# Half of the early tokens' first layer in seven products, and a new order of small transfers, in a routed-expert kernel

## The chip, the cores and the metric

The kernel runs on one core of a Trainium2 chip. The metric is device microseconds (us) of one execution; the kernel before took 435.68 us (median of 3 runs, 435.34 to 438.09). The profile names the engines PE (TensorE: matmuls and transposes), PEld (its weight loads), DVE (VectorE), ACT (ScalarE), POOL (GpSimd) and SP (SyncE, which only starts transfers). Each engine works through its own instructions in a fixed order; a `q` behind a name (SPq) is that engine's queue of transfers.

## The reference

Two blocks follow one another. The first is a linear attention with decay over 4 batches, 8 heads, 768 positions and head size 64, in blocks of positions with a running state. Its output is laid out as 3072 tokens of 512 numbers. The second sends each token to one of 8 experts:

```python
logits = x @ w_gate
expert_idx = np.argmax(logits, axis=1)
...
for e in range(E):
    mask = expert_idx == e
    ...
    xe = x[mask]
    h = np.maximum(xe @ w1[e], 0.0)      # 512 -> 1024
    ye = h @ w2[e]                       # 1024 -> 512
    out[mask] = gate_w[mask, None] * ye
```

All of it is in float32. The number of tokens of each expert is known only when the attention has run.

## The kernel before, in words

**Attention.** Twelve steps: six blocks of 128 positions, times two pairs of batches. Each step turns q and k, forms scores, outputs and the new state on PE, and turns the outputs into rows of tokens that go to `xs` in DRAM (`store_rows`). One step later the step's tokens are routed: `leave` forms logits, `choose` (line 397 on) finds on DVE the best expert (`mx`, `sh`, `key`, `pick`, `oh`), `ranks` (line 441) counts on PE, with the matrix `oh`, how many tokens before a given one chose the same expert, `put` turns that into a place on the expert's list (`place`, `slot`, `slot_i`), and POOL writes an entry at that place of `slots` in DRAM (`store`, line 467): one indirect transfer for 128 tokens. These transfers wait in the list `waiting` until `store_places` issues some.

**Early tokens.** Expert 5 (`FIRST`) is begun before the lists are complete. After two thirds of the routing, POOL reads the first 256 places of its list (`list_0a`), and `gather_early` fetches those 256 rows of `xs` into `xg` with two indirect transfers. A manual dependency (`hold`) keeps the first of them until PE has done the step's scores. SP's load of the expert's second weight matrix `w2t` waits for both gathers; its `w1t` was loaded ahead in two halves.

**The experts' passes.** Pass 0 is these 256 tokens; pass 1 ("0b") is the rest of expert 5, up to 128 tokens; passes 2 to 8 are the other seven experts, in an order that depends on how many tokens each has, so that SP reads the expert's number (`turns`, made on DVE) before it can load list and weights. In each pass, tokens are turned into `xgT` (128 partitions x 4 pieces x tokens; PE transposes and a copy in passes 0 and 1, `turn`, and for the others 16-bit planes made on ACT, transposed by the DMA engines from SP's queue, and copied together again on ACT, `split` and `join`). The first layer is `hidden` (line 606: 8 blocks of 128 outputs, each four matmuls over the four pieces) for passes 0 and 1. From pass 2 on it is `hidden_fast`: a product of 2x2 blocks with seven block products instead of eight (Strassen's form, with 4 sums of weight blocks made on POOL, `s_...`, 4 sums of token blocks made on DVE, `t_...`, and sums of the products on DVE). The second layers are in seven products as well (lines 774, 782 and 914). In pass 0 DVE makes the sums of `w2t` (`second_sums`, line 683) and those of `hT` (lines 752 to 755).

**Order.** The instructions are put into each engine's order by a scheduler that estimates times; those wrapped in `pin` keep the order in which they are written. Buffers come from pools with a fixed number of rooms for a name: there is one room for `xgT`, so that the `xgT` of pass 2 can only be written when pass 1's first layer has read its own.

Of the kernel before, what the change touches and what calls it, by code (L numbers as in the profile page):

```python
# [10 lines left out]
F32 = mybir.dt.float32  # L11
# [11 lines left out]
def kernel(  # L23
# [207 lines left out]
    def pin(inst):  # L231
        tc.keep_in_program_order(inst)
        return inst
# [270 lines left out]
    def at(m, t):  # L504

        w = m.widths[t]
        return m.ids[:w, t, 0:1], m.ids[:w, t, 1:2], m.list[:w, t, 2:3]
# [76 lines left out]
        for u in range(2):  # L584
            pin(nc.scalar.copy(to[:, u], m.across[u][:, :, :m.n]))

    def turn(m, pin=lambda inst: inst):
        m.xgT = ffn.tile([P, DC, m.n], F32, tag="xgT", name="xgT", bufs=1)
        for c in range(0, DC, 2):
            tp = bank(next(tp_banks), [P, 2, m.n], "tp")  # L590
            for dc, (t, w) in itertools.product(range(c, c + 2), enumerate(m.widths)):
                pin(nc.tensor.transpose(tp[:, dc - c, t * P:t * P + w],
                                        m.xg[t // 2][:w, t % 2, dc * P:(dc + 1) * P],
                                        ident[:w, :w]))

# [15 lines left out]

    DH, FH = DC // 2, F // 2

    def form(product, sums_of, temps, give, first=nothing):

        a, b = sums_of
        p1, u2, u3 = temps
        pin(nc.scalar.copy(p1, product(a.a11, b.b11)))  # L618
        first()
        pin(nc.vector.tensor_add(u2, product(a.s2, b.t2), p1))  # L620
        pin(nc.vector.tensor_add(u3, product(a.s3, b.t3), u2))
        p5 = product(a.s1, b.t1)
        give(1, 1, p5, u3)
        nc.vector.tensor_add(u2, p5, u2)
        give(0, 0, product(a.a12, b.b21), p1)
        give(0, 1, product(a.s4, b.b22), u2)
        give(1, 0, product(a.a22, b.t4), u3)

    def form_early(product, sums_of, temps, give, ahead):

        a, b = sums_of
        p1, u2, u3, u4 = temps
        nc.vector.tensor_copy(p1, product(a.a11, b.b11))
        give(0, 0, product(a.a12, b.b21), p1)
        nc.vector.tensor_add(u2, product(a.s2, b.t2), p1)
        nc.vector.tensor_add(u3, product(a.s3, b.t3), u2)
        p5 = product(a.s1, b.t1)
        give(1, 1, p5, u3)
        nc.vector.tensor_add(u4, p5, u2)
        give(0, 1, product(a.s4, b.b22), u4)  # L640
        ahead()
        give(1, 0, product(a.a22, b.t4), u3)

    def right_sums(b, t1, t2, t3, t4, sub):
# [9 lines left out]
    def pool_sub(o, x, y):  # L654
        return nc.gpsimd.tensor_tensor(out=o, in0=x, in1=y, op=ALU.subtract)  # L655
# [130 lines left out]
    def pair_rooms():  # L786
        o = [o_room[:, next(o_slots)] for i in range(2)]
        outs = [[o[i][:, k * MD // 2:(k + 1) * MD // 2] for k in range(2)] for i in range(2)]
        u = x_room[:, next(x_slots)].rearrange("p b (i n) -> p (b i) n", i=2)
        return o, outs, [u[:, i, :] for i in range(4)]  # L790

    def outputs_early(m, w2, ahead):
        a = left_of(m.hT, 0, P, pair_rooms_of_sums())
        for make in (a.s3_made, a.s1_made, a.s2_made, a.s4_made):
            make()
        o, outs, temps = pair_rooms()

        def give(i, k, p, u):
            gate = at(m, i)[2]
            nc.vector.tensor_scalar_mul(outs[i][k], u, gate)  # L800
            nc.vector.scalar_tensor_tensor(out=outs[i][k], in0=p, scalar=gate, in1=outs[i][k],
                                           op0=ALU.mult, op1=ALU.add)

        form_early(block, (a, w2), temps, give, ahead)
        for i in range(2):
            scatter(at(m, i)[1], o[i])

    def lone_tile(m, i, b, banks):

# [325 lines left out]
    def gather_early(other):  # L1135

        m, w2t = passes[0], weights[0][1]
        pin(nc.gpsimd.memset(between, 0.0))
        begun = fetch(m, 1 + (NSTEP - 2) * B * C, pin)
        hold(begun[0], other)  # L1140
        behind = nc.sync.dma_start(out=w2t, in_=w2_r[FIRST])
        pin(behind)
        for other in begun:
            tc.add_manual_dep(behind.ins, other.ins.name, mybir.DependencyInfo(
                mybir.DependencyClass.Sync, mybir.DependencyReason.DATA),
                reason="the gathers have the DMA engines first")
# [15 lines left out]
        nc.gpsimd.tensor_copy(gates[1][halves[u]], gates[0][halves[1 - u]])  # L1162
    for i in range(len(steps)):
        rest = leave(last, (4, 6, 7) if i < len(steps) - 1 else (4, 2, 3)) if last else nothing

        ahead = (enter(i + 1, rest, stores(i))
                 if 0 < i < len(steps) - 1 else None)
        if ahead:
            if last:
                with tc.issue_after(ahead.copied.ins):  # L1170
                    store_rows(last)
        elif last:
            store_rows(last)
# [12 lines left out]
        to_sbuf(cur)  # L1186
        if cur.n == NSTEP - 1:
            if ahead:
                for s in range(2):
                    score(ahead, s)  # L1190
                gather_early(ahead.scored)
# [12 lines left out]
        for group in ranked:  # L1204
            give_places(group)
        if 0 < i < 3:
            empty_lists(i - 1)
        if ahead and i < len(steps) - 3:
            fade(ahead)
            store_places(1 if i < 5 else 2)  # L1210
        last, cur = cur, ahead
# [47 lines left out]
                           engines=[mybir.EngineType.SP])  # L1259
        passes.append(make_pass(e, 0, CAPS[i], str(i)))  # L1260

    passes.append(make_pass(FIRST, EARLY, CAPS[0] - EARLY, "0b"))
    next_pass(1)
    later = []
    weights.append(load_weights(passes[2].w, later))
    for m in passes[1:]:
        fetch(m)
    last = E
    for i in range(last + 1):
        m = passes[i]  # L1270
        w1t, w2t = weights[max(i - 1, 0)]
        ahead = passes[i + 1] if 0 < i < last else None


        def beside():
            if ahead:
                split(ahead)
                if later:
                    with tc.issue_after(ahead.turning.ins):
                        later.pop()()  # L1280

        def between():
            if waiting_rows:
                waiting_rows.pop()()

        if i == 0:
            w2 = second_sums(w2t, vector_sub)
        if i < 2:
            hidden(m, w1t)
        elif i < last:  # L1290
            w2 = across_sums(w2t)
            hidden_fast(m, w1, beside, lambda: between() or token_halves(m))
        else:
            w2 = second_sums(w2t, pool_sub_last)
            tc.keep_in_program_order(nc.gpsimd.drain())
            hidden_fast(m, w1, beside, between, TG * P)
            later_sums(m)
        if i == 0:
            split(passes[2])
            with tc.issue_after(passes[2].turning.ins):  # L1300
                for j in range(2, E):
                    next_pass(j)
            later.pop()()
        if ahead:
            w1, finish = first_sums(weights[i][0])
        if 0 < i < last - 1:
            fetch(passes[i + 2], pin=pin)
        if i == 0:
            outputs_early(m, w2, lambda: turn(passes[1], pin))
# [58 lines left out]
```

## Time and profile before

| what | us |
|---|---|
| median of 3 runs | 435.68 (435.34 to 438.09) |
| the profiled execution | 435.07 |
| its span, first to last instruction | 432.8 |
| PE busy | 421.3 (97%) |
| DVE, POOL, ACT busy | 266.0, 257.5, 176.8 |
| routing of the last steps and early first layer on PE | 118 to 140 |
| second layer of pass 0, first layer of pass 1 | 140 to 159.7 |
| second layer of pass 1 | 159.7 to 167.8 |
| passes 2 to 8 | 167.8 to 407, then a tail to 432.8 |

The times in this table and in the rows below are those of the profiled execution, counted from its first instruction. A matmul in float32 appears in the trace as two records, so "x56" of line 606 is 28 matmuls. PE's granted clock is 1.00 in all stretches from 107 to 407 us, which is the higher of its two levels (2.4 GHz).

### The profile page before, as it was taken

Reading aid. Unit: us, or ns where it says so; the run is one execution under the profiler, and the core shown is the slowest. Engines: PE = TensorE matmul, PEld = TensorE weight load, DVE = VectorE, ACT = ScalarE, POOL = GpSimd, SP = SyncE. Lnnn points to the kernel's source line nnn. Section 1 sums busy time; section 2 is a strip of 40 time slices with the busy share of each in tenths; the row PEclk is TensorE's granted clock in tenths of the full one; section 3 lists DMA queues with packets and bytes.
Section 4 is the critical chain, followed back from the end, with each engine's and each line's share of the span. In section 5 each row is a group of like instructions: output and inputs, shape, how many; then the busy total and the mean of one; then the engine's idle time right before and its main releaser. Section 6 shows DMA issues by size and latency. Waiting matters only on the chain.

```text
span 432.8 us, 9573 instructions
## 1 busy us (share of the span) xinstructions
PE 421.3 (97%) x3699; PEld 393.9 (91%) x3699; DVE 266.0 (61%) x585; ACT 176.8 (41%) x319; POOL 257.5 (59%) x205
## 2 busy tenths in 40 slices
PE   8999999999999999999999999999999999999993
PEld 6888898888888897999999999999999999999972
DVE  6656656566766647686547757755575664775463
ACT  3366545555542423450554155245424605422221
POOL 5243457373344368777948757693885887749032
PEclk9999999999999999999999999999999999999998
DMA  9999989999985758976369857965975894753122
GB/s 174 211 245 229 220 213 213 233 193 249 292 283 149 265 105 234 325 246 237 52 139 190 332 76 157 319 179 112 299 246 81 196 384 80 153 186 56 20 83 63
DMA packets 164727, 83.49 MB, mean 193 GB/s; under 512 B 146019, under 2 KB 146063, under 8 KB 164672
## 3 DMA queue, kind: packets, MB, share of 16 engines
q1 hardware_dynamic: 155024, 63.21, 61.2%
q0 software_dynamic: 5712, 13.26, 10.2%
q10 hardware_dynamic: 3936, 6.31, 4.2%
q8 instruction: 31, 0.51, 0.5%
q14 instruction: 24, 0.20, 0.2%
HBM read 58.96 MB, written 13.09 MB: 166 GB/s over the span
## 4 chain that ended last, share of the span: by engine, by line
PE 87%; DMA 4%; issue 3%; ACT 2%; POOL 1%; SPq 1%; DVE 1%; POOLq 0%; ACTq 0%
PE p L728 30%; PE p L914 26%; PE sp L279 5%; PE ph L606 5%; PE op L314 4%; PE p L774 3%; DMA v_in<-in_v_dram 3%; PE cp L340 2%; PE tx L376 2%; PE tk L241 2%; PE tq L241 2%; PE op L305 2%; PE p L782 2%; PE lgT L366 1%; DMA xg<-xs,list_0a 1%
## 5 line engine op out<-in xcount | busy, mean ns | idle before, releaser
L533 POOL DMA_INDIRECT out_dram<-o_room,list x24 | 25.7, 1069 | 51.9 <-DMA decay<-planes_q 22.4
L286 DVE TENSOR_TENSOR mt<-sp,decay 128x512 f32<-128x512 f32 x48 | 30.1, 684 | 23.8 <-PE sp L279 18.6
L739 ACT ACTIVATE hT<-hT 128x418 f32<-128x418 f32 (+6 forms) x56 | 28.3, 521 | 34.1 <-DVE hT L736 31.2
L728 PE MATMUL p<-xgT,w1t 128*128 128x209 f32 (+6 forms) x224 | 41.4, 327 | 0.0
L728 PEld LDWEIGHTS p<-xgT,w1t 128*128 128x128 f32 x224 | 37.1, 189 | 0.8 <-issue 0.8
L618 ACT COPY u_qT<-p 128x418 f32<-128x418 f32 (+6 forms) x14 | 6.7, 479 | 69.5 <-PE p L728 69.5
L914 PE MATMUL p<-hT,w2t 128*128 128x209 f32 (+5 forms) x192 | 33.6, 328 | 0.0
L914 PEld LDWEIGHTS p<-hT,w2t 128*128 128x128 f32 x192 | 32.0, 189 | 0.0
L467 POOL DMA_INDIRECT slots<-entry,slot_i x24 | 23.8, 990 | 13.1 <-PE tl L391 5.9
L527 POOL DMA_INDIRECT xg<-xs,list x25 | 25.9, 1034 | 9.0 <-issue 6.1
L736 DVE TENSOR_TENSOR hT<-p,u_kd 128x418 f32<-128x418 f32 (+6 forms) x28 | 15.6, 559 | 21.0 <-PE p L728 21.0
L279 PE MATMUL sp<-qT,kT 64*128 64x128 f32 x384 | 27.5, 293 | 0.4 <-ACT kT L263 0.4
L279 PEld LDWEIGHTS sp<-qT,kT 64*128 64x128 f32 x384 | 24.3, 199 | 3.0 <-issue 2.0
L269 POOL TENSOR_TENSOR kd<-k_in,kdec 128x512 f32<-128x512 f32 x12 | 12.4, 1042 | 23.7 <-PE cp L340 11.9
L655 POOL TENSOR_TENSOR s_q<-w1t 128x1024 f32<-128x1024 f32 x7 | 16.5, 2363 | 16.6 <-DVE t_xT L713 14.6
L326 ACT COPY xT<-op 128x512 f32<-128x512 f32 x12 | 7.0, 585 | 36.9 <-PE op L314 33.8
L606 PE MATMUL ph<-xgT,w1t 128*128 128x256 f32 (+1 forms) x128 | 21.6, 328 | 0.0
L606 PEld LDWEIGHTS ph<-xgT,w1t 128*128 128x128 f32 x128 | 19.2, 191 | 1.7
L728 PE MATMUL p<-t_sd,w1t 128*128 128x209 f32 (+6 forms) x112 | 20.7, 327 | 0.0
L728 PE MATMUL p<-st,s_q 128*128 128x209 f32 (+6 forms) x112 | 20.7, 327 | 0.0
L652 POOL TENSOR_TENSOR w1t<-w1t 128x1024 f32<-128x1024 f32 x7 | 20.2, 2892 | 0.6
L728 PE MATMUL p<-t_xT,w1t 128*128 128x209 f32 (+6 forms) x112 | 20.6, 326 | 0.0
(252 smaller groups left out, 1093.9 us busy)
## 6 DMA issues: line engine op xcount, KB each, us to landing
w2t<-in_moe_w_dram SPq DMA_DIRECT2D x8, 2048.0 KB
w1t<-in_moe_w_dram SPq DMA_DIRECT2D x7, 2048.0 KB
xs<-x_room ACTq DMA_DIRECT2D x12, 512.0 KB
v_in<-in_v_dram SPq DMA_DIRECT2D x8, 512.0 KB
o_room<-qs_room SPq DMA_DIRECT2D x76, 48.0 KB
q_in<-in_q_dram SPq DMA_DIRECT2D x7, 512.0 KB
k_in<-in_k_dram SPq DMA_DIRECT2D x7, 512.0 KB
room<-in_q_dram SPq DMA_DIRECT2D x4, 512.0 KB
```

Of the source, the lines that this page charges most:

```text
L241: pin(nc.tensor.transpose(t[:, i, b, :], src[:, b, h:h + 2, :], ident))
L279: m.scored = pin(nc.tensor.matmul(sp[u][:, i, b, :], lhsT=m.kT[s][halves[u], i, b, :], rhs=m.qT[s][halves[u], i, b, :], start=(i == 0 and ...
L286: nc.vector.tensor_mul(mt[:, u], sp[u], decay[:, u, s * HP // 2:(s + 1) * HP // 2].unsqueeze(2).to_broadcast(shp))
L314: pin(nc.tensor.matmul(out_at(m, b, u, hp), lhsT=m.v[:, b, 2 * hp + u, :], rhs=m.mt[hp // 2][:, u, hp % 2, b, :], start=(first and hp == 0 ...
L467: put = nc.gpsimd.indirect_dma_start(out=slots, out_offset=bass.IndirectOffsetOnAxis(ap=slot_i[:, i:i + 1], axis=0), in_=entry[:, n, bs[i] ...
L527: return nc.gpsimd.indirect_dma_start(out=dst, out_offset=None, in_=xs[:rows, :], in_offset=bass.IndirectOffsetOnAxis(ap=idx, axis=0))
L533: put = nc.gpsimd.indirect_dma_start(out=out, out_offset=bass.IndirectOffsetOnAxis(ap=idx, axis=0), in_=src, in_offset=None, bounds_check= ...
L606: nc.tensor.matmul(ph, lhsT=w1t[:, dc, fc * P:(fc + 1) * P], rhs=m.xgT[:, dc, :], start=(dc == 0), stop=(dc == DC - 1))
L652: return nc.gpsimd.tensor_tensor(out=o, in0=x, in1=y, op=ALU.add)
L728: nc.tensor.matmul(p[:, i, :], lhsT=lhs[:, dc, g, i * P:(i + 1) * P], rhs=rhs[:, dc, :], start=(dc == 0), stop=(dc == DH - 1))
L739: pin(nc.scalar.activation(outs[i][k], outs[i][k], ACT.Relu))
L914: nc.tensor.matmul(p[:, c, :], lhsT=lhs[:, f, c * P:(c + 1) * P], rhs=rhs[:, f, :], start=(f == 0), stop=(f == FC // 2 - 1))
```

## The change

It does five things. (1) In pass 0, the upper four of the eight blocks of 128 outputs of the first layer are formed by `hidden_early` as seven products of 2x2 blocks; the lower four stay as they were. The four sums of weight blocks, 128x512 each (`e_q`, `e_k`), are made on POOL by `early_sums`: one behind the early gathers, three in the last attention step. The four sums of token blocks, 128x256 each, are made on DVE. The four sums of `w2t` on DVE now stand one by one between the steps of the products (`others`). (2) The early gathers are no longer held. (3) Two of the list entries' transfers (`store_places(2)`) are issued in the last attention step. (4) SP reads the list of pass 2 before that of 0b, and POOL gathers the tokens of pass 2 before those of 0b; all these are pinned. (5) The `xgT` of 0b lies in a room of its own, `short_room`, and `outputs_early` has another order of products, with a bank named for each. The second expert's `w1t` is one transfer of 2048 KB, as before.

```diff
@@ turn
-    def turn(m, pin=lambda inst: inst):
-        m.xgT = ffn.tile([P, DC, m.n], F32, tag="xgT", name="xgT", bufs=1)
+    def turn(m, pin=lambda inst: inst, room=None):
+        m.xgT = room
+        if room is None:
+            m.xgT = ffn.tile([P, DC, m.n], F32, tag="xgT", name="xgT", bufs=1)
...
+    def early_sums(w1t):
+        w = w1t.rearrange("p (j d) (g i f) -> p i j d g f", j=2, g=2, i=2)
+        a = [[w[:, i, j, :, 1] for j in range(2)] for i in range(2)]
+        q, k = (qkv.tile([P, 2, DH, FH // 2], F32, tag=t, name=f"e_{t}") for t in "qk")
+        s1, s2, s3, s4 = q[:, 0], q[:, 1], k[:, 0], k[:, 1]
+        pin(pool_sub(s3, a[0][0], a[1][0]))
+        def others():
+            pin(pool_add(s1, a[1][0], a[1][1]))
+            pin(pool_sub(s2, s1, a[0][0]))
+            pin(pool_sub(s4, a[0][1], s2))
...
+    def hidden_early(m, w1t, a, others):
...
+        for fc in range(FC // 2):
...
+            relu(1, m.hT[:, fc, :], ph)
...
+        b = right_sums(b, t1, t2, t3, t4, vector_sub)
...
+        x1 = product(a.a11, b.b11, 0)
+        pin(nc.scalar.copy(p1, x1))
+        x7 = product(a.s2, b.t2, 1)
+        ready(0, 0, product(a.a12, b.b21, 0, x1))
+        others.pop(0)()
+        add(u2, x7, p1)
+        x3 = product(a.s3, b.t3, 2)
+        others.pop(0)()
+        add(u3, x3, u2)
+        x6 = product(a.a22, b.t4, 3)
+        others.pop(0)()
+        add(outs[1][0], x6, u3)
+        ready(1, 0)
+        x5 = product(a.s1, b.t1, 6)
+        add(outs[1][1], x5, u3)
+        ready(1, 1)
+        add(u4, x5, u2)
+        others.pop(0)()
+        add(outs[0][1], product(a.s4, b.b22, 1), u4)
+        ready(0, 1)
...
@@ outputs_early
+        a.s1_made()
+        a.s2_made()
+        pin(nc.vector.tensor_copy(p1, block(a.a11, b.b11, 7)))
+        a.s3_made()
+        a.s4_made()
+        give(0, 0, block(a.a12, b.b21, 4), p1)
+        p6 = block(a.a22, b.t4, 5)
+        add(u2, block(a.s2, b.t2, 7), p1)
+        add(u3, block(a.s3, b.t3, 4), u2)
+        give(1, 0, p6, u3)
+        p5 = block(a.s1, b.t1, 7)
+        give(1, 1, p5, u3)
+        add(u4, p5, u2)
+        scatter(at(m, 1)[1], o[1])
+        ahead()
+        give(0, 1, block(a.s4, b.b22, 4), u4)
+        scatter(at(m, 0)[1], o[0])
...
@@ gather_early
         begun = fetch(m, 1 + (NSTEP - 2) * B * C, pin)
-        hold(begun[0], other)
+        m.sums = early_sums(weights[0][0])
...
@@ the loop over the attention's steps
+        if i == len(steps) - 1:
+            pin(nc.gpsimd.memset(between, 0.0))
+            store_places(2)
+            passes[0].sums.others()
...
-    passes.append(make_pass(FIRST, EARLY, CAPS[0] - EARLY, "0b"))
     next_pass(1)
+    passes.insert(1, make_pass(FIRST, EARLY, CAPS[0] - EARLY, "0b"))
...
-    for m in passes[1:]:
-        fetch(m)
+    for m in passes[:0:-1]:
+        fetch(m, pin=pin)
```

The order on POOL at the early gathers, before (`between` is one column that is only written to keep transfers apart, `slots` are the list entries' transfers):

```order
L467 DMA slots<-entry,slot_i 27648x4
L1138 MEMSET between 128x1
L527 DMA xg<-xs,list_0a 128x512 x2
L1064 MEMSET between 128x1
L467 DMA slots<-entry,slot_i 27648x4
```

And now:

```order
L527 DMA xg<-xs,list_0a 128x512 x2
L716 TENSOR_TENSOR e_k<-w1t 128x512
L1240 MEMSET between 128x1
L467 DMA slots<-entry,slot_i 27648x4
L1124 MEMSET between 128x1
L467 DMA slots<-entry,slot_i 27648x4
L713 TENSOR_TENSOR e_q<-w1t 128x512
L716 TENSOR_TENSOR e_q<-e_q,w1t 128x512
L716 TENSOR_TENSOR e_k<-w1t,e_q 128x512
```

Before, six transfers of entries followed the gathers without a break; now two of them stand ahead of three sums, and four behind them.

The order on POOL at the gathers of passes 1 (`list_0b`) and 2, before:

```order
L1050 MEMSET between 128x1
L467 DMA slots<-entry,slot_i 27648x4 x2
L527 DMA xg<-xs,list_0b 128x512
L527 DMA xg<-xs,list_2270 128x512 x3
L527 DMA xg<-xs,list_2270 48x512
```

And now:

```order
L1124 MEMSET between 128x1
L467 DMA slots<-entry,slot_i 27648x4 x2
L527 DMA xg<-xs,list_2274 128x512 x3
L527 DMA xg<-xs,list_2274 48x512
L527 DMA xg<-xs,list_0b 128x512
```

The gather of 0b went from the front to the end; SP's reads of the two lists changed places in the same way.

The order on DVE behind the last small step of the routing (`beyond`), before:

```order
L1254 TENSOR_REDUCE beyond<-beyond 128x1
L683 TENSOR_TENSOR t_q<-w2t 128x1024
L683 TENSOR_TENSOR t_v<-w2t 128x1024
L683 TENSOR_TENSOR t_k<-w2t,t_q 128x1024
L683 TENSOR_TENSOR t_m<-w2t,t_k 128x1024
L752 TENSOR_TENSOR h_sd<-hT 128x512
```

And now:

```order
L1332 TENSOR_REDUCE beyond<-beyond 128x1
L744 TENSOR_TENSOR e_sd<-xgT 128x256 x2
L744 TENSOR_TENSOR st<-xgT,e_sd 128x256
L744 TENSOR_TENSOR e_xT<-xgT,st 128x256
L744 TENSOR_TENSOR t_q<-w2t 128x1024
L664 TENSOR_TENSOR u_kT<-pe,u_qT 128x256
L744 TENSOR_TENSOR t_v<-w2t 128x1024
L664 TENSOR_TENSOR u_kd<-pe,u_kT 128x256
L744 TENSOR_TENSOR t_k<-w2t,t_q 128x1024
L664 TENSOR_TENSOR hT<-pe,u_kd 128x2x128 x2
L664 TENSOR_TENSOR u_2328<-pe,u_kT 128x256
L744 TENSOR_TENSOR t_m<-w2t,t_k 128x1024
```

Four sums of token blocks came in front, and sums of the products (`pe`) between the sums of `w2t`.

## Rows read from the trace of the kernel before

**Rows 1.** The page, its first part: the span, and the busy time of PE.
```profile
span 432.8 us, 9573 instructions
PE 421.3 (97%) x3699; PEld 393.9 (91%) x3699; DVE 266.0 (61%) x585; ACT 176.8 (41%) x319; POOL 257.5 (59%) x205
```
**Rows 2.** Busy time by stretch: its bounds, its length, then busy us (and instructions) of PE, PEld, DVE, ACT, POOL; then the granted clock of PE, the DMA engines' share and GB/s.
```profile
118.00:128.00 10.00, 9.87 (x138) 7.81 (x138) 6.02 (x32) 5.51 (x16) 3.65 (x6) 1.00 0.86 285
128.00:140.00 12.00, 12.00 (x57) 10.58 (x56) 8.18 (x29) 2.41 (x7) 6.14 (x10) 1.00 0.56 173
...
187.60:407.00 219.40, 219.40 (x1347) 219.37 (x1346) 138.07 (x229) 82.87 (x128) 154.98 (x84) 1.00 0.69 184
```
**Rows 3.** The chain of work that ended last, in order of time: start, length, what.
```profile
127.03 0.23 PE rank L441 x3
...
127.81 12.19 PE ph L606 x56
152.53 7.14 PE ph L606 x64
...
166.33 0.35 issue
```
**Rows 4.** Timeline of PEld and PE: start, length, instruction, and in brackets the idle time before it and what ended it.
```profile
122.70 0.75 PEld L592 LDWEIGHTS tp<-ident,xg 128*128 128x128 f32 x7 [0.31 <-DMA xg<-xs,list_0a]
127.03 0.10 PEld L441 LDWEIGHTS <-before 128*128 128x128 bf16 x1 [0.46 <-DVE oh L417]
112.42 1.97 PE L314 MATMUL op<-mt,v_in 128*64 128x128 f32 x32
119.15 1.97 PE L314 MATMUL op<-mt,v_in 128*64 128x128 f32 x32
```
**Rows 5.** Timeline of POOL around the early gathers and the list entries.
```profile
113.50 0.12 POOL L1138 MEMSET between<- 128x1 f32 x1
117.72 1.00 POOL L527 DMA_INDIRECT xg<-xs,list_0a  x1 [4.10 <-PE rank L441]
125.96 1.00 POOL L467 DMA_INDIRECT slots<-entry,slot_i  x1 [5.85 <-PE tl L391]
132.33 0.96 POOL L467 DMA_INDIRECT slots<-entry,slot_i  x1 [0.30 <-issue]
```
**Rows 6.** Timeline of DVE in the routing of the last two steps.
```profile
119.56 0.43 DVE L465 CAST slot_i<-slot 128x2 int32<-128x2 f32 x1
123.02 0.17 DVE L402 TENSOR_TENSOR sh<-lg,mx 128x16 f32<-128x16 f32 x1
124.30 0.18 DVE L417 TENSOR_TENSOR oh<-key,pick 128x16 bf16<-128x16 f32 x1
124.71 0.17 DVE L422 TENSOR_TENSOR so_far<-so_far,new 128x8 bf16<-128x8 bf16 x1
125.00 0.17 DVE L426 TENSOR_SCALAR sm<-sm 128x2 f32<-128x2 f32 x1
125.72 0.23 DVE L393 TENSOR_REDUCE lg<-tl 128x16 f32<-128x64 f32 x1 [0.35 <-PE tl L391]
126.80 0.17 DVE L417 TENSOR_TENSOR oh<-key,pick 128x16 bf16<-128x16 f32 x1
```
**Rows 7.** Timelines of POOL and DVE at two places where both work on SBUF: a POOL instruction, and the DVE instruction that meets it.
```profile
73.07 1.03 POOL L269 TENSOR_TENSOR kd<-k_in,kdec 128x512 f32<-128x512 f32 x1 [2.35 <-issue]
73.09 1.04 DVE L422 TENSOR_TENSOR so_far<-so_far,new 128x8 bf16<-128x8 bf16 x1
178.19 2.37 POOL L652 TENSOR_TENSOR w2t<-w2t 128x1024 f32<-128x1024 f32 x1
179.07 2.37 DVE L895 TENSOR_TENSOR t_mt<-hT 128x836 f32<-128x836 f32 x1 [0.62 <-ACT hT L739]
```
**Rows 8.** Groups of POOL by line: count, busy us and mean ns.
```profile
L655 POOL TENSOR_TENSOR s_v<-w1t,s_q 128x1024 f32<-128x1024 f32 x7 | 16.5, 2361 | 0.5
```
**Rows 9.** Timeline of DVE in pass 0: sums of the second weights, and a sum of a product.
```profile
133.90 1.23 DVE L683 TENSOR_TENSOR t_q<-w2t 128x1024 f32<-128x1024 f32 x1 [2.77 <-DMA w2t<-in_moe_w_dram]
141.18 0.69 DVE L754 TENSOR_TENSOR h_kT<-h_qT,hT 128x512 f32<-128x512 f32 x1
145.22 0.42 DVE L635 TENSOR_TENSOR x_room<-p,x_room 128x256 f32<-128x256 f32 x1 [1.08 <-issue]
```
**Rows 10.** Timelines of SP's queue, POOL and ACT on the way to the tokens of passes 1 and 2.
```profile
135.15 0.34 SPq L496 DMA_DIRECT2D list_0b<-slots  x1
136.83 0.38 SPq L202 DMA_DIRECT2D w1t<-in_moe_w_dram  x1
139.81 0.97 POOL L527 DMA_INDIRECT xg<-xs,list  x1 [0.30 <-issue]
146.70 2.18 ACT L575 COPY planes_q<-xg 128x512 uint16<-128x512 uint16 x4 [6.28 <-DMA xg<-xs,list]
```
**Rows 11.** Timelines of ACT, DVE, POOL and PE at the passage from pass 1 to pass 2.
```profile
159.75 2.09 ACT L585 COPY xgT<-decay 128x1672 uint16<-128x1672 uint16 x1 [8.31 <-PE ph L606]
165.57 0.59 DVE L713 TENSOR_TENSOR t_xT<-xgT,st 128x418 f32<-128x418 f32 x1
166.41 2.38 POOL L655 TENSOR_TENSOR s_q<-w1t 128x1024 f32<-128x1024 f32 x1
168.86 1.66 PE L728 MATMUL p<-st,s_q 128*128 128x209 f32 x8
```

More of the change, by code (lines that the diff above doesn't have):

```diff
@@ L612 @@
     DH, FH = DC // 2, F // 2
+    def early_sums(w1t):
[8 more added lines that the diff above has]
+            pin(pool_sub(s4, a[0][1], s2))
+        return SimpleNamespace(a11=a[0][0], a12=a[0][1], a22=a[1][1], s1=s1, s2=s2, s3=s3, s4=s4,
+                               others=others)
@@ new lines, in hidden_early, with product, add, ready @@
+    def hidden_early(m, w1t, a, others):
+        h = m.n // 2
+        m.hT = ffn.tile([P, FC, m.n], F32, tag="hT", name="hT", bufs=1)
+        for fc in range(FC // 2):
+            ph = bank(next(ph_banks), [P, m.n], "ph")
+            for dc in range(DC):
+                nc.tensor.matmul(ph, lhsT=w1t[:, dc, fc * P:(fc + 1) * P], rhs=m.xgT[:, dc, :],
+                                 start=(dc == 0), stop=(dc == DC - 1))
+            relu(1, m.hT[:, fc, :], ph)
+        b = [[m.xgT[:, j * DH:(j + 1) * DH, k * h:(k + 1) * h] for k in range(2)] for j in range(2)]
+        t1, t3, t4 = (work.tile([P, DH, h], F32, tag=t, name=f"e_{t}", bufs=n)
+                      for t, n in (("sd", 2), ("sd", 2), ("xT", 1)))
+        t2 = st.rearrange("p b g d -> p (b g d)")[:, :DH * h].rearrange("p (c n) -> p c n", c=DH)
+        b = right_sums(b, t1, t2, t3, t4, vector_sub)
+        p1, u2, u3 = thirds(h)
+        u4 = work.tile([P, 2, h], F32, tag="kT", name="u_4")
+        c = FC // 2
+        outs = [[m.hT[:, c + 2 * i:c + 2 * i + 2, k * h:(k + 1) * h] for k in range(2)]
+                for i in range(2)]
+        def product(lhs, rhs, at, onto=None):
+            p = bank(at, [P, 2, h], "pe") if onto is None else onto
+            for i in range(2):
+                for dc in range(DH):
+                    pin(nc.tensor.matmul(p[:, i, :], lhsT=lhs[:, dc, i * P:(i + 1) * P],
+                                         rhs=rhs[:, dc, :], start=(onto is None and i == dc == 0),
+                                         stop=(i == 1 and dc == DH - 1),
+                                         skip_group_check=True))
+            return p
+        def add(*x):
+            pin(nc.vector.tensor_add(*x))
+        def ready(i, k, src=None):
+            pin(nc.scalar.activation(outs[i][k], outs[i][k] if src is None else src, ACT.Relu))
+        x1 = product(a.a11, b.b11, 0)
[18 more added lines that the diff above has]
+        ready(0, 1)
@@ L626, in form @@
         give(0, 1, product(a.s4, b.b22), u2)
[L627 to L641, printed above, removed]
         give(1, 0, product(a.a22, b.t4), u3)
@@ L790, in pair_rooms, with outputs_early @@
         return o, outs, [u[:, i, :] for i in range(4)]
-    def outputs_early(m, w2, ahead):
+    def outputs_early(m, b, ahead):
         a = left_of(m.hT, 0, P, pair_rooms_of_sums())
-        for make in (a.s3_made, a.s1_made, a.s2_made, a.s4_made):
-            make()
-        o, outs, temps = pair_rooms()
+        o, outs, (p1, u2, u3, u4) = pair_rooms()
+        add = nc.vector.tensor_add
         def give(i, k, p, u):
@@ L802, in give @@
                                            op0=ALU.mult, op1=ALU.add)
-        form_early(block, (a, w2), temps, give, ahead)
-        for i in range(2):
-            scatter(at(m, i)[1], o[i])
+        a.s1_made()
[15 more added lines that the diff above has]
+        scatter(at(m, 0)[1], o[0])
     def lone_tile(m, i, b, banks):
@@ L1133, in start_early, with gather_early @@
         passes.append(make_pass(FIRST, 0, EARLY, "0a", pin, nc.gpsimd))
-    def gather_early(other):
+    def gather_early():
         m, w2t = passes[0], weights[0][1]
@@ L1190 @@
                     score(ahead, s)
-                gather_early(ahead.scored)
+                gather_early()
             else:
@@ L1260, in next_pass @@
         passes.append(make_pass(e, 0, CAPS[i], str(i)))
[L1262 removed]
     next_pass(1)
+    passes.insert(1, make_pass(FIRST, EARLY, CAPS[0] - EARLY, "0b"))
+    short_room = qs_room[:, 2].rearrange("p i b c -> p (i b) c")
     later = []
     weights.append(load_weights(passes[2].w, later))
[L1266 to L1267 removed]
+    for m in passes[:0:-1]:
+        fetch(m, pin=pin)
     last = E
@@ L1286 @@
         if i == 0:
-            w2 = second_sums(w2t, vector_sub)
-        if i < 2:
+            others = []
+            w2 = second_sums(w2t, lambda *x: others.append(lambda: vector_sub(*x)))
+            hidden_early(m, w1t, m.sums, others)
+        elif i < 2:
             hidden(m, w1t)
@@ L1308 @@
         if i == 0:
-            outputs_early(m, w2, lambda: turn(passes[1], pin))
+            outputs_early(m, w2, lambda: turn(passes[1], pin, short_room))
         elif i == 1:
```

## The prediction, made before the changed kernel was timed

> **What bounds the kernel now.** The page's first part comes first: PE is busy for 421.3 of 432.8 us [rows 1]. The table by stretch shows where it is not a little but wholly full: 12.00 of 12.00 us in 128 to 140, all of 187.6 to 407, and 9.87 of 10.00 in 118 to 128, always at a granted clock of 1.00 [rows 2]. So what is taken off PE between 118 and 168 moves everything behind it, one to one, and what makes PE wait there is paid in full. The chain of waits [rows 3] confirms it: from 127 to 168 it is PE's own work, with one gap of 0.35 at 166.33. The timelines of PE's weight loads [rows 4] then name what it waits for in the routing: 0.31 for the early gathers at 122.70, and DVE's `oh` at 127.03, which comes just in time. This last one matters most below: DVE finishes the second `oh` at 126.97 [rows 6] and PE starts to count at 127.03, so DVE has no time to spare there.
>
> **Seven products.** Removed are 16 matmuls of 256 columns, 32 records. 56 such records take 12.19 us [rows 3], 0.218 each: 6.97 us. Added are 7 x 4 = 28 matmuls of 128 columns, 56 records; 64 of that size take 7.14 us [rows 3], 0.112 each: 6.25 us. On PE this is -0.72 us. The cover: DVE gets four sums of 128x256, at about 0.42 each [rows 9] 1.7 us, which fit into its idle 2.77 us ahead of `t_q` [rows 9]. PE reaches the products after 12 more matmuls from 127.81, at 133.0; the second product needs three of these sums, done by about 132.4. The four sums of `w2t` (1.23 each) and six sums of products (0.42 each) are 7.4 us on DVE, against 6.25 us of products and 5.2 us of second-layer blocks (12 matmuls of 0.435) that PE has before the first block that needs a sum of `hT`. With the last relu and two sums `h_` at 0.69 [rows 9] DVE is done at about 143, PE asks at 144.5. I cost this at nothing; without that 1.5 us each us of DVE would be one of PE.
>
> **Early gathers.** Held until 117.72, POOL had been ready since 113.62 [rows 5]. PE's wait of 0.31 goes, at best. That transfers in flight slow PE's short products is not seen: the same 32 matmuls take 1.97 us at 112.42 without the gathers and 1.97 at 119.15 beside them [rows 4]. `w2t` follows the gathers, some 4 us earlier; that only ends DVE's wait for it.
>
> **Sums on POOL.** One costs 2.361 / 2 = 1.18 us (half the elements of [rows 8]). The first follows the gathers and is done before the next entries can be stored, unless `w1t`'s first half is late. Then two entries follow DVE's `slot_i` of 119.99 [rows 6], from about 120.3 to 122.5 (1.3 us apart [rows 5]); so the three other sums run from about 122.6 to 126.3. That is the very stretch in which DVE chooses the experts. Where both engines read SBUF, DVE's instruction is held: `so_far` took 1.04 us instead of 0.17 and ended with POOL's `kd`; `t_mt`, a float32 sum, took 2.37 and ended 0.88 after POOL's [rows 7]. No row shows `sh`, `key` or the first `oh` beside POOL, so I bound the cost. Low: only the forms like `so_far` and the scaling `sm` are held. `sm`, due at 125.00, meets the third sum and ends at 126.3; the next `lg` starts at 126.6 instead of 125.72, as 0.35 of idle time absorbs a part [rows 6]: +0.85 for PE at 127.03. High: every DVE instruction with two inputs in SBUF is held. `sh` ends at 123.8, `key` at 125.1, `oh` at 126.3 instead of 124.48; 0.9 of work follows, and `lg` starts at 127.27: +1.55. I take 1.2, the middle, since the start of the sums is uncertain by as much as one sum. The gathers' 0.31 is swallowed by this wait, as PE waits later for DVE anyway.
>
> The Trainium skill (SBUF — State Buffer, section SBUF: two separate sides) says that VectorE and GpSimd share one pair of SBUF ports as an exclusive lock: a VectorE instruction with two SBUF inputs is blocked by a GpSimd instruction that reads SBUF for all of it. By that rule the high end holds, and the sum below would be +0.48 instead of +0.13. The trace agrees for `so_far` and `t_mt` [rows 7]; for the three instructions in question no row shows it.
>
> **Transfers moved.** Four entries instead of six stand behind 125.96 [rows 5], so the last is out about 2 us before 132.33, and SP's read of a list about 2 us before 135.15 [rows 10]; pass 2's list and gathers gain 1.9 us more by going first. Its tokens arrived at 146.70, 6.9 us after their gather behind 2 MB of `w1t` [rows 10], and should come 2 to 3 us earlier. 0b's gather, now last, is issued at about 141.5 and should land by 148.5; PE needs it at about 149.5. Cost nothing, with 1 us to spare. If DVE's chain is 1.2 late, half of the 2 us goes, and PE's need moves too.
>
> **Own room for 0b.** ACT waited 8.31 us for PE's reading of `xgT` [rows 11]. Without that wait the join starts when the transposes have landed, some 2 us earlier, and DVE's token sums end before PE asks: the gap of 0.35 goes [rows 3]. A second bound lies here: PE began the product with `s_q` at 168.86, and POOL ended `s_q` at 168.79 [rows 11]. PE can be earlier only if that chain (list, planes, transposes, gathers, `s_q`) is earlier too, which the moved transfers must bring.
>
> **Sum.** -0.72 - 0.35 + 1.2 = +0.13 us, between -0.22 and +0.48. On the profiled 435.07 this is 435.2; the median of the runs stood 0.61 above that execution, so I forecast 435.8: no change.
>
> **The rivals.**
> - *Faster: POOL's sums don't meet DVE's chain.* They would have to run before 122.6 or slip past DVE's small instructions; for it: DVE's instructions at 0.17 us leave gaps between POOL's. Against it: the order puts the sums behind two entries that need 119.99. Then -0.72 - 0.35 - 0.31 = -1.4: 434.3. Chance 0.25.
> - *Slower: POOL keeps the ports.* If DVE's `sh` gets no turn between the three sums, it ends at 126.3 instead of 123.19, 3.1 late; the idle 0.35 gives back some, and PE counts 2.8 late: 2.8 - 1.07 = +1.7, 437.4. It decides from the point at which a sum starts at the end of the one before it. Against it: `t_mt` ran as soon as POOL's first instruction was done [rows 7]. Chance 0.11.
> - *DVE becomes the bound of the products*, if the sums of `w2t` start late or each sum of a product waits behind one: 1 to 2 us beyond its cover, about 437. Chance 0.05.
> - *The transfers come no earlier*, so that the change does not do what it says: PE then meets `s_q` at 168.86 as before, whatever it saved: 435.7. Chance 0.05.
> - Something else, of either sign: 0.04.
>
> **The numbers.** The forecast has 0.50. Its own range is 435.4 to 436.3 with the bounds above. The range from 434.1 to 437.3 takes in the faster rival and most of the slower cases, and 0.3 for the runs' scatter (435.34 to 435.68 in two of three). A measurement of this kernel can tell about 1% (4.4 us) from no change; no case with a worked price reaches that, so: faster by over 1% 0.02, within 1% 0.95, slower by over 1% 0.03.
>
> **What would show it.** In the changed profile: 56 records of 0.112 us in the products without idle time before them; the early gathers at about 114; POOL's three sums beside `sh`, `key`, `oh`, with one or more of these at 0.5 to 1.2 us, and a wait of PE for `oh` of about 1 us in all; pass 2's planes at 144 to 145.5; no gap before the last four matmuls of pass 1. I am wrong if `sh` and `oh` stay at 0.17 us beside POOL (then 434.3), if PE waits inside the products, or if the transposes of 0b wait for their gather.

## The result: slower by half a percent, and the profile after

The changed kernel takes 436.51 us (median of 22 runs, 434.98 to 440.30), the kernel before 434.43 beside it (22 runs, 432.82 to 438.09). The ratio is 1.0054, with a 95% interval of 1.0039 to 1.0069: about 2.3 us more, within the 1% of "no change". The profiled execution took 436.42 us with a span of 434.6; that of before took 435.07 with 432.8.

The page's first part, to be read against [rows 1]: PE is busy for 4.0 us less, POOL for 7.9 more and DVE for 7.5 more.

```profile
span 434.6 us, 9647 instructions
PE 417.3 (96%) x3723; PEld 391.5 (90%) x3723; DVE 273.5 (63%) x595; ACT 177.0 (41%) x320; POOL 265.4 (61%) x209
```

The table by stretch, columns as in [rows 2]. PE lost 2.58 of 10 us in 118 to 128, where it had lost 0.13; the later stretches are as full as before, at the same granted clock.

```profile
118.00:128.00 10.00, 7.42 (x117) 5.97 (x110) 6.42 (x17) 4.53 (x13) 7.97 (x10) 1.00 0.87 272
128.00:140.00 12.00, 11.76 (x79) 10.52 (x78) 9.86 (x46) 2.68 (x8) 4.62 (x7) 1.00 0.31 90
...
187.60:407.00 219.40, 219.40 (x1346) 219.40 (x1345) 138.60 (x229) 83.35 (x129) 156.10 (x85) 1.00 0.68 184
```

PE's timeline of the changed kernel names what it waits for; the waits for `oh` had been foreseen, the one for `xT` had not. The last line is the first product with `s_q` in pass 2's first layer, where [rows 11] had PE at 168.86.

```profile
120.56 1.10 PE L305 MATMUL op<-qs_room,st 64*64 64x128 f32 x32
...
121.87 1.04 PE L594 MATMUL tp<-ident,xg 128*128 128x128 f32 x8
124.44 0.66 PE L376 MATMUL tx<-ident,xT 128*128 128x128 f32 x4 [1.54 <-ACT xT L326]
...
127.30 0.18 PE L441 MATMUL rank<-oh,before 128*128 128x16 bf16 x1 [1.04 <-DVE oh L417]
...
129.34 0.18 PE L441 MATMUL rank<-oh,before 128*128 128x16 bf16 x1 [0.24 <-DVE oh L417]
...
170.28 1.68 PE L789 MATMUL p<-st,s_q 128*128 128x209 f32 x8 [0.38 <-POOL s_q L716]
```

ACT and DVE show that the first wait is an odd one. `xT` needs only the `op` products, and those end at 121.66 (120.56 + 1.10); `lg` needs `tl`, done at 122.03. Both readers start at 123.8. ACT's timeline of the changed kernel, with the copies of the second expert's tokens as its last line, 1.14 us later than in [rows 10]:

```profile
123.80 0.58 ACT L326 COPY xT<-op 128x512 f32<-128x512 f32 x1 [3.55 <-PE tp L594]
...
147.84 2.18 ACT L575 COPY planes_q<-xg 128x512 uint16<-128x512 uint16 x4 [4.36 <-issue]
```

DVE's timeline of the changed kernel; `place`, `key` and `oh` took 0.16 to 0.18 us before:

```profile
118.45 1.58 DVE L458 TENSOR_TENSOR place<-rank_in,ebase_late 128x16 f32<-128x16 f32 x1
...
123.85 0.23 DVE L393 TENSOR_REDUCE lg<-tl 128x16 f32<-128x64 f32 x1 [3.20 <-PE tp L594]
...
124.31 0.24 DVE L402 TENSOR_TENSOR sh<-lg,mx 128x16 f32<-128x16 f32 x1
...
125.08 0.83 DVE L407 SCALAR_TENSOR_TENSOR key<-sh,rev 128x16 f32<-128x16 f32 x1
...
126.14 1.10 DVE L417 TENSOR_TENSOR oh<-key,pick 128x16 bf16<-128x16 f32 x1
```

POOL's timeline of the changed kernel, to be read against [rows 5]. The gathers come only 1.3 us earlier, since their list is now what they wait for. The two moved entries stand between `e_k` and the three sums, and the last entry (133.77) is 1.4 us later than before.

```profile
116.41 1.00 POOL L527 DMA_INDIRECT xg<-xs,list_0a  x1 [3.29 <-DMA list_0a<-slots]
117.71 0.97 POOL L527 DMA_INDIRECT xg<-xs,list_0a  x1 [0.30 <-issue]
118.69 1.30 POOL L716 TENSOR_TENSOR e_k<-w1t 128x512 f32<-128x512 f32 x1
...
120.93 1.01 POOL L467 DMA_INDIRECT slots<-entry,slot_i  x1 [0.90 <-DVE slot_i L465]
...
122.24 0.97 POOL L467 DMA_INDIRECT slots<-entry,slot_i  x1 [0.19 <-issue]
123.24 1.27 POOL L713 TENSOR_TENSOR e_q<-w1t 128x512 f32<-128x512 f32 x1
124.59 1.28 POOL L716 TENSOR_TENSOR e_q<-e_q,w1t 128x512 f32<-128x512 f32 x1
125.95 1.26 POOL L716 TENSOR_TENSOR e_k<-w1t,e_q 128x512 f32<-128x512 f32 x1
...
133.77 1.03 POOL L467 DMA_INDIRECT slots<-entry,slot_i  x1 [0.30 <-issue]
```

**Where the time went.** The starts of a few PE instructions cut both traces into the same pieces (us; `tq` is its last matmul in that step, the last column runs to the span's end; the names are PE's tiles):

| trace | tq to tp | tp to tx | tx to rank | rank to cnt | cnt to 0b's tp | 0b's tp to s_q | to the end |
|---|---|---|---|---|---|---|---|
| before | 10.58 | 1.16 | 1.66 | 2.45 | 22.56 | 18.66 | 263.97 |
| changed | 10.58 | 2.58 | 2.86 | 2.64 | 21.91 | 18.43 | 264.34 |
| difference | 0 | +1.42 | +1.20 | +0.19 | -0.65 | -0.23 | +0.37 |

Together +2.30, which is what the runs show (the two spans differ by 1.8 only, as `tq` comes 0.49 us earlier in the changed kernel). The last column is taken for scatter: the one kernel of the experiments that was profiled twice has 263.64 and 263.37 there, and all traces together have 263.37 to 264.92.

### The profile page after: what moved, and what is told of

It is laid out like the page before. It is cut to its first block, busy times and chain, and to the rows that moved or that the text cites. A ratio compares the mean times of both kernels' runs of the same rounds, so it can differ in the third digit from the quotient of the medians.

```text
span 434.6 us, 9647 instructions
## 1 busy us (share of the span) xinstructions
PE 417.3 (96%) x3723; PEld 391.5 (90%) x3723; DVE 273.5 (63%) x595; ACT 177.0 (41%) x320; POOL 265.4 (61%) x209
## 4 chain that ended last, share of the span: by engine, by line
PE 86%; SPq 4%; DMA 2%; issue 1%; POOL 1%; DVE 1%; ACT 1%; POOLq 0%; DVEq 0%
PE p L789 29%; PE p L988 26%; PE p L835 5%; PE op L314 5%; PE sp L279 4%; PE op L305 2%; PE tx L376 2%; PE cp L340 2%; PE tk L241 2%; DMA k_in<-in_k_dram 2%; PE tq L241 2%; SPq L116 2%; PE p L843 1%; PE pe L657 1%; SPq L577 1%
## 5 line engine op out<-in xcount | busy, mean ns | idle before, releaser
L527 POOL DMA_INDIRECT xg<-xs,list x25 | 28.7, 1148 | 12.9 <-DMA list<-slots 6.7
L279 PE MATMUL sp<-qT,kT 64*128 64x128 f32 x384 | 25.8, 281 | 0.7 <-issue 0.7
L279 PEld LDWEIGHTS sp<-qT,kT 64*128 64x128 f32 x384 | 22.8, 187 | 3.1 <-issue 2.7
L789 PE MATMUL p<-xgT,s_v 128*128 128x209 f32 (+6 forms) x112 | 20.5, 326 | 0.0
L789 PE MATMUL p<-xgT,s_k 128*128 128x209 f32 (+6 forms) x112 | 20.5, 326 | 0.0
```

The costliest lines, as they stand in the source:

```text
L279: m.scored = pin(nc.tensor.matmul(sp[u][:, i, b, :], lhsT=m.kT[s][halves[u], i, b, :], rhs=m.qT[s][halves[u], i, b, :], start=(i == 0 and ...
L527: return nc.gpsimd.indirect_dma_start(out=dst, out_offset=None, in_=xs[:rows, :], in_offset=bass.IndirectOffsetOnAxis(ap=idx, axis=0))
L789: nc.tensor.matmul(p[:, i, :], lhsT=lhs[:, dc, g, i * P:(i + 1) * P], rhs=rhs[:, dc, :], start=(dc == 0), stop=(dc == DH - 1))
```

## The experiments

Two theories at first. **P**: POOL's sums hold DVE's routing, the 1.39 us of `tx` to `cnt`. **G**: the gathers, no longer held, put `w2t`'s load and themselves beside PE's short products, the 1.42 of `tp` to `tx`. Each kernel was timed beside the kernel before; the first four ran on one chip, the next four on a second, the last four on a third. The record does not name the chip of the changed kernel's own runs.

**The three sums left out.**

```diff
+        s1 = s2 = s3 = s4 = k[:, 0]
...
-            pin(pool_add(s1, a[1][0], a[1][1]))
-            pin(pool_sub(s2, s1, a[0][0]))
-            pin(pool_sub(s4, a[0][1], s2))
```

> The changed kernel without the three sums on POOL (S1, S2, S4 of the early first layer's left side); S3 stands in for all four, so half of the early tokens' hidden values are not the reference's. Theory P (the sums on POOL hold DVE's routing): key and oh fall from 0.83 and 1.10 us to 0.17, TensorE's wait for oh at the first rank product (1.04 us) falls under 0.3, the puts behind them start about 3 us earlier, and the ratio to before falls from 1.005 to about 1.002 (435.2 where before takes 434.4). The 1.5 us wait of TensorE for xT behind the early tokens' transposes stays. Theory G (all of the loss is that the gathers are no longer held, so that w2t's load begins beside TensorE's short products): the ratio stays at 1.005, the wait for oh moves elsewhere.

433.44 us beside 433.61, ratio 0.9997 (0.9981 to 1.0014): by this ratio and the change's 1.0054, each good to some 0.7 us, the sums are worth 2.4 us of the change. `key` takes 0.17 and `oh` 0.18, and PE waits for neither. The drop is larger than P's 1.39 us, and its profiled execution, the longest of the twelve (435.30), lost 2.57 us at another place: PE stood still inside `op` (L305) while gathers ran from 113.03 to 115.30.

**The gathers held again**, and **both at once**.

```diff
+        hold(begun[0], other)
```

> The changed kernel with the early gathers held behind the step's score products again, as in the kernel before. Theory G: TensorE's 1.5 us wait for xT is gone (0 to 0.3), DVE's lg follows the tl transposes by less than 0.6 us, and the ratio to before is about 1.002. Theory P: lg comes 1.2 us sooner but the sums then begin 1.3 us later as well and meet the same sh, key and oh, so the wait for oh stays at 1 us or grows, the ratio is 1.002 to 1.004. If the wait for xT was a thing of that one execution, the ratio stays at 1.005.

> Both at once: the gathers held, and the three sums left out (S3 stands in for them, half of the early tokens' hidden values are wrong). If P and G are the two causes and add up, the loss is gone: routing ends as in the kernel before, the products' 0.65 us and the gap in pass 1 are gained, and the ratio is 0.997 to 0.999. If a third cause is in the later transfers, the ratio stays above 1.001.

Held: 435.46, ratio 1.0046 (1.0027 to 1.0064), not told apart from the change's 1.0054. G falls: the wait is still there, in PE's timeline of the held kernel.

```profile
122.93 0.66 PE L376 MATMUL tx<-ident,xT 128*128 128x128 f32 x4 [1.15 <-ACT xT L326]
```

Both: 433.70, ratio 1.0005 (0.9989 to 1.0021). With the gathers held the sums are worth 1.8 us, but the kernel is no faster than before, though the products give 0.65: it still waits 1.26 us for `xT`. A third cause is left. In all three traces so far with this wait (changed, held, both) two list entries run on POOL just then, and `xT` or `lg` starts 0.5 to 0.6 us after the second has ended (changed: 122.24 + 0.97 = 123.21, then 123.80).

**The later transfers as before** (puts behind the last step, lists and room as before; sums and unheld gathers stay).

```diff
-            store_places(2)
...
-    passes.insert(1, make_pass(FIRST, EARLY, CAPS[0] - EARLY, "0b"))
...
-    for m in passes[:0:-1]:
-        fetch(m, pin=pin)
+    for m in passes[1:]:
+        fetch(m)
```

> The changed kernel with the second expert's transfers, the room of the late tokens' rows and the last puts as in the kernel before; the Strassen half with its sums on POOL and the unheld gathers stay. If the moved transfers cost nothing (as predicted), the ratio stays at 1.004 to 1.006, with the 0.35 us gap in pass 1 back. If the puts in front of the sums delay the sums into DVE's routing, the sums begin about 2 us earlier here (right behind e_k, 119.9 instead of 123.2), hit other instructions than key and oh, and the ratio falls to about 1.002.

435.34, ratio 1.0034 (1.0014 to 1.0053). The wait for `xT` is gone, and the sums, now from 118.19 on, hold `place` and `slot_i` instead of `key` and `oh`, so that PE does not wait for `oh`: from `tx` to `cnt` it takes 4.12 us, as before (4.11). In their place PE loses 1.1 us earlier, behind the unheld gathers of 114.66 and 115.96. PE's timeline of this kernel:

```profile
117.71 0.65 PE L366 MATMUL lgT<-xT,gates 128*32 128x128 f32 x16 [1.04 <-ACT rank_in L447]
```

So a third theory, **B**: beside an indirect transfer that POOL issues, PE's results reach their readers late. It is in the trace of before as well. PE's timeline of the kernel before:

```profile
118.56 0.66 PE L376 MATMUL tx<-ident,xT 128*128 128x128 f32 x4
```

Its POOL, with the second early gather:

```profile
119.02 0.97 POOL L527 DMA_INDIRECT xg<-xs,list_0a  x1 [0.31 <-issue]
```

And its ACT, which reads what `tx` wrote:

```profile
120.58 0.65 ACT L379 COPY x_room<-tx 128x256 f32<-128x256 f32 x2 [1.11 <-PE tx L376]
```

`tx` ends at 119.22 and ACT reads it at 120.58, 0.59 after the gather's end. It cost nothing there, as PE needed nothing of ACT until 123.5.

**The kernel before with the two puts moved, alone.**

```diff
+        if i == len(steps) - 1:
+            pin(nc.gpsimd.memset(between, 0.0))
+            store_places(2)
```

> The kernel before with one part of the change alone: the two puts of list entries stand ahead of the last attention step, as in the change. Theory B (two indirect transfers that POOL issues one behind the other keep TensorE's results from the engines that wait for them, until about 0.6 us behind the second): ACT's xT behind the op products starts 1.2 to 2 us after those products end in place of 0.1, TensorE waits for xT 1.0 to 1.6 us behind the early tokens' transposes, and the ratio is 1.002 to 1.004. Rival (the stall belongs to the sums or to w2t's load): no wait over 0.3 us there, ratio 0.999 to 1.001.

436.24 beside 433.94, ratio 1.0063 (1.0039 to 1.0087, six runs): the moved puts alone cost as much as the whole change. Not in the way that I had expected: it is not `tx` that waits, PE itself creeps through `op`, with nothing that it waits for by the profile. PE's timeline of this kernel:

```profile
119.64 1.01 PE L305 MATMUL op<-qs_room,st 64*64 64x128 f32 x8
120.92 0.45 PE L305 MATMUL op<-qs_room,st 64*64 64x128 f32 x5 [0.26 <-issue]
121.64 0.27 PE L305 MATMUL op<-qs_room,st 64*64 64x128 f32 x1 [0.27 <-issue]
122.37 0.85 PE L305 MATMUL op<-qs_room,st 64*64 64x128 f32 x18 [0.46 <-issue]
```

32 matmuls take 3.58 us instead of 1.10; POOL's second put ended at 121.55.

**The kernel before with the gathers not held, alone.**

```diff
-        hold(begun[0], other)
```

> The kernel before with the early gathers not held, alone. Theory B: the gathers come at 113 to 116.5, as soon as their list has landed, and TensorE's results are late there (sp or rank, 115 to 117.5): 0.5 to 2.5 us of TensorE's idle time before the early transposes in place of none, 0.31 us less at the transposes; ratio 1.000 to 1.004, with more spread than the kernel before. Theory of the prediction: the gathers' earlier start costs nothing, ratio 0.999 to 1.0005.

434.65, ratio 1.0013 (0.9993 to 1.0032): too little to tell. Its trace has the gathers at 113.50 and 1.22 us more from `tq` to `tp`, and 0.29 less from `tp` to `tx`.

**The sums on DVE**, in the time in which it waits for PE; then the same **with gathers and puts as before**.

```diff
-        pin(pool_sub(s3, a[0][0], a[1][0]))
...
+            sub = nc.vector.tensor_sub
+            pin(sub(s3, a[0][0], a[1][0]))
+            pin(nc.vector.tensor_add(s1, a[1][0], a[1][1]))
...
```

> The changed kernel with all four early sums on DVE, behind slot_i and ahead of lg, where DVE waits for TensorE; puts and gathers as in the change. Theory P: four sums of 0.6 to 0.7 us end before or just after lg's transposes, key and oh take 0.17, TensorE's wait for oh is gone, ratio 0.999 to 1.001, as with the sums left out (0.9997). Rival (the sums cost the same wherever they stand, as DVE is the bound of this stretch): lg starts 1 us or more late, ratio 1.003 or more.

> The same with the gathers held again and the two puts behind the last step, as in the kernel before. If the sums on POOL, the puts and the unheld gathers are all of the loss, routing runs as in the kernel before, the products are shorter (0.65 us) and the gap in pass 1 is gone: ratio 0.997 to 0.999. If the ratio stays at 1.000 or above, something in the later part (lists, gathers of the second expert, products' adds) costs as much as the products give.

A sum takes 0.69 us on DVE; in both traces all four end before PE has what `lg` needs. The first: 434.64, ratio 1.0017 (0.9985 to 1.0050). The second: 433.46 beside 433.94, ratio 1.0010 (0.9984 to 1.0036), median and mean on opposite sides of 1. In its trace routing is as before (11.64 us from `tq` to `tx`, before 11.74) and 0b's stretch 0.66 shorter; but the stretch of the products is as long as before (22.58 us), 0.41 of it a wait of PE for ACT's copy of the first product. That copy is late in the same way: the ACT instruction ahead of it reads at 134.03 what PE had ended at 132.53, with the last entry on POOL until 132.94.

**On the third chip**: sums on POOL right behind the held gathers; sums on DVE with the gathers held and the puts moved; the last kernel of above again; and the kernel before with its early gathers issued twice.

```diff
+        twice = ffn.tile([P, 2, MD], F32, tag="xg", name="xg_twice", bufs=4)
+        for t in range(2):
+            pin(gather(twice[:, t, :], m.ids[:, t, 0:1], 1 + (NSTEP - 2) * B * C))
```

> The changed kernel with the early gathers held and the two puts behind the last step, sums on POOL right behind the gathers: what the sums cost where nothing else of POOL stands in the way. Theory P: e_k and the first sum hold place, slot_i (119 to 121) and the last two hold sh, key, oh or new by 0.8 to 1.2 us each; TensorE waits for oh 0.7 to 1.5 us; ratio 1.000 to 1.003. Rival (all is the indirect transfers' doing): ratio as with the sums on DVE, 0.997 to 1.000.

> Sums on DVE, early gathers held, the two puts ahead of the last step as in the change: what the puts cost where no sum holds DVE. Theory B: gathers at 117 to 120 and puts at 120.3 to 123 follow each other, TensorE's results due from 121.5 on come out 0.6 us behind the second put, TensorE idles 1 to 1.6 us at tx or inside the op products; ratio 1.001 to 1.005, at least 0.003 above the kernel with the puts back. Rival: no such wait, ratio equal to the kernel with the puts back.

> The same kernel as e8_dve_held_puts_back once more, beside the kernel before on this chip, for a narrower interval: 0.997 to 1.000 if its median of 433.46 beside 433.94 was the truth, 1.001 to 1.003 if its mean was.

> The kernel before with the two early gathers issued a second time, into a room that nobody reads; nothing else is moved, no sum, no put. Theory B (any indirect transfer that POOL issues beside short products does it): the second pair ends at 122.6 and TensorE's results due from 121 on come out at 123.1 to 123.3, 1.0 to 1.3 us late; ratio 1.002 to 1.004. Rival (it is the puts into the lists, or their wait for DVE, not the issue of indirect transfers): no wait over 0.4 us, ratio 0.999 to 1.001.

434.11, 433.24, 433.65 and 433.43 beside 434.00: ratios 0.9999 (0.9969 to 1.0028), 0.9972 (0.9942 to 1.0001), 0.9995 (0.9963 to 1.0026) and 0.9998 (0.9961 to 1.0036). None differs from the kernel before. B predicted a loss for the second and the fourth, and missed; for the first, P had a wait of 0.7 to 1.5 us for `oh`, and it is 0.23. In the fourth, four indirect transfers run without a pause, the last from 118.68 to 119.63, and ACT has `xT` 0.07 us after `op` has ended (118.17 + 1.10 = 119.27). ACT's timeline of this kernel:

```profile
119.34 0.59 ACT L326 COPY xT<-op 128x512 f32<-128x512 f32 x1 [2.32 <-PE op L305]
```

The kernel that ran on both chips shows what differs. On the second chip, the product of `lgT` (117.54, 0.65) ends at 118.19, beside a gather from 118.57 to 119.55; ACT reads it 1.89 us later, by its timeline:

```profile
120.08 0.37 ACT L1166 COPY parts<-lgT 128x256 f32<-128x256 f32 x1 [1.84 <-PE tx L376]
```

On the third, `lgT` (115.49, 0.64) ends at 116.13 and the gather runs from 116.73 to 117.70; ACT, by its timeline there, reads it 0.08 us later:

```profile
116.21 0.37 ACT L1166 COPY parts<-lgT 128x256 f32<-128x256 f32 x1
```

In these four traces no result of PE that was due between 45 and 140 us came more than 0.15 us late; in the other ten traces results did, by up to 2.3 us (held kernel: `op` done at 120.02, read at 122.29), beside indirect transfers. What PE waits for in the four is the gathers' landing, 0.67, 1.39, 0.99 and 0.88 us at `tp`, where it was 0.31 before. So the second of them takes 13.67 us from `tq` to `tx` all the same: what B had wrong there is the cause of the wait, and the ratio.

Two more things can be read from the traces' records of signals (the semaphore updates by which one instruction tells another that it is done). PE's signal itself is late, not its reader: in the changed kernel, those of the four products that end from 121.66 to 122.90 all stand between 123.78 and 123.94, while on the third chip that of `lgT` above stands at 116.18, right behind its end. And the four traces share more than the chip: their records are nearly complete. Of about 5000 signals by which transfers report their landing, these four hold 4973 to 5022, the other ten 4258 to 4403, and the pages of the ten give no time to landing. The page of the kernel that ran on both chips, on the second:

```profile
w2t<-in_moe_w_dram SPq DMA_DIRECT2D x8, 2048.0 KB
```

And on the third:

```profile
w2t<-in_moe_w_dram SPq DMA_DIRECT2D x8, 2048.0 KB, 9.3
```

The chip and the completeness of the recording changed together, and no run separates them. Each timed run has a span and a granted clock on record, so none of them shows whether PE's signals come late in an execution that is not recorded.

Of the sums on POOL the third chip shows this: right behind the gathers they hold DVE longer than in the change, but mostly where PE does not wait for it, or waits for the gathers anyway (0.67 us at `tp`). DVE's timeline of the kernel with the sums on POOL:

```profile
116.79 3.03 DVE L465 CAST slot_i<-slot 128x2 int32<-128x2 f32 x1
...
120.25 0.91 DVE L402 TENSOR_TENSOR sh<-lg,mx 128x16 f32<-128x16 f32 x1
...
121.72 0.80 DVE L407 SCALAR_TENSOR_TENSOR key<-sh,rev 128x16 f32<-128x16 f32 x1
...
122.76 0.18 DVE L417 TENSOR_TENSOR oh<-key,pick 128x16 bf16<-128x16 f32 x1
```

From `tx` to `cnt` this kernel takes 4.29 us, 0.18 more than before; the change took 1.39 more, and the kernel with the later transfers as before, whose sums also follow the gathers at once, 0.01 more. P stands as a mechanism; its price is set by where the sums stand and by what else PE waits for.

## Why the prediction was right, and which step was wrong

The time (436.51 for 435.8, in the range) and the call of no change held. For the time this was luck: the sum forecast +0.13 and the runs show +2.3, but the sum was added to a median of three runs, 435.68, that lay 1.25 above that of the 22 runs beside the changed kernel, 434.43. From that base the same sum gives 434.6 and the same range ends at 436.1, below what was measured; the forecast's own range, 435.4 to 436.3, was missed as it stands. The call of no change at 1% did not need this luck. The steps:

- **Seven products**, -0.72: measured -0.65, 56 records in 6.25 us without idle time before them. DVE covered its work, as costed.
- **Early gathers**: nothing was gained, as said, but they did not come at 114: POOL was free at 113.1 and waited for the list's landing until 116.41. PE's 0.31 at the gathers went, and was lost again in the wait for `xT`. "That transfers in flight slow PE's short products is not seen" was read from the wrong quantity. The matmuls' pace at 119.15 [rows 4] was unchanged; the time until a result beside them was read was not (`tx`, done at 119.22, read at 120.58).
- **Sums on POOL**, +1.2 between 0.85 and 1.55: measured +1.39 (1.20 to the first rank, 0.19 behind it), by the mechanism named. `key` and `oh` end 0.04 and 0.03 us after the sum beside them; `sh` was caught by a sum's last 0.2 us only. The rule cited from the Trainium skill (SBUF — State Buffer, section SBUF: two separate sides) agrees with each of these three. The measured price lies 0.19 above my middle and 0.16 below the high end.
- **Transfers moved**, cost 0, list and planes 2 to 3 us earlier: this is the step that failed, twice. Beside the puts the changed kernel lost 1.42 us of PE, and moved alone they cost the kernel before about 2.3 us, where PE's results come late; on the third chip, where they don't, the kernel with the puts moved was no slower (0.9972). And nothing came earlier: the list was read at 136.64, the planes started at 147.84, 1.14 later than in [rows 10]. I counted two puts fewer at the end but not that the rest of POOL's entries stand behind the sums, and these behind the puts, and that DVE, which gives the entries, was late itself.
- **Own room for 0b**, -0.35: the gap is gone, the join no longer waits for PE's reading but for its transposes; the passage got 0.61 us shorter, of which PE lost 0.38 to the second bound that was named, `s_q`: -0.23.
- **Sum**: +0.13 was forecast. The foreseen terms measured -0.65 + 1.39 - 0.23 = +0.51; the term that was set to zero added 1.42, and 0.37 is taken for scatter.

The rival "DVE becomes the bound of the products" did not come about, nor did "POOL keeps the ports" for `sh`. "The transfers come no earlier" had 0.05; its condition came true, but PE, late itself, met `s_q` at 170.28 and not at 168.86.

What stays open: why PE's signals come late beside POOL's transfers, and why not in the four traces of the third chip: whether it is the chip, the recording or something else that these four share. The changed kernel is not among the four. The prices of the parts don't add up either: the puts cost 2.3 us alone and the sums 2.4 (1.8 with the gathers held), more than the change's 2.3 and the 0.9 that it gained. Each is good to 0.7 to 1.0 us, and the two waits may hide one another in part; no run shows it. That sums on DVE, held gathers and late puts beat the kernel before is not shown: 433.46 and 433.65 beside 433.94 and 434.00, with both intervals around 1.

## What to carry to other kernels

Before moving a small transfer into a stretch of short products, look in the trace for the time between a product's end and its reader's start beside transfers of the same kind; the pace of the products need not show it. When work is put on an idle engine, count the place of everything behind it in that engine's queue, and choose the place by which instructions of the other engine it will hold: the same sums cost 0.0 to 0.2 us of PE from `tx` to `cnt` right behind the gathers and 1.4 behind two more entries. Time a gain of under a percent on more than one chip, and look whether the traces that are compared are equally complete.

## What the runs showed that was not expected

Beside POOL's indirect transfers PE's finished results were read up to 2.3 us late (changed: `op` done at 121.66, read at 123.80; the kernel profiled on two chips: 1.89 us on the one, 0.08 on the other). In the cases shown from before, the change, the held kernel and the second chip the readers start 0.5 to 0.6 us after the end of a transfer instruction on POOL; elsewhere also beside one (gathers not held: `xT` read at 115.57, the second gather from 114.80 to 115.77). Where PE had enough short products in hand, PE itself came to a halt (3.58 us for 1.10 of `op`).

A DVE instruction that POOL holds may miss the turn between two sums: `slot_i`, with one small input, took 3.03 us over the whole of the first two sums, while `key` and `oh` got theirs after one. POOL's timeline of that kernel has the second sum begin as the first ends (117.23 + 1.30 = 118.53); the sums beside `key` and `oh` in the change stand 0.08 us apart. That this gap decides is argued from two cases (the other is `place`, 1.49 us, with the later transfers as before) and not tested.

```profile
117.23 1.30 POOL L716 TENSOR_TENSOR e_k<-w1t 128x512 f32<-128x512 f32 x1
...
118.49 1.29 POOL L713 TENSOR_TENSOR e_q<-w1t 128x512 f32<-128x512 f32 x1
```
